# Order of the triples' last products, and another path for two units' transposed k, in an HGRN2 + SwiGLU kernel

## The chip, the cores and the metric

The kernel runs on one core of a Trainium2 chip. The metric is the device time of one execution in microseconds (us), the median of several runs. A profiled execution on the same chip gives the views that are quoted below; its times count from the start of its span. Engines are named PE (TensorE matmuls), PEld (TensorE weight loads), DVE (VectorE), ACT (ScalarE), POOL (GpSimd) and SP (SyncE, which issues DMAs here).

## The reference, cut to what matters

```python
B, H, S, D = 4, 8, 768, 48           # batch, heads, sequence, head size
f = sigmoid(f_logit)
for t in range(S):                   # attention: a decayed state for each head
    state = f[:, :, t, :, None] * state + einsum('bhd,bhe->bhde', k[:, :, t], v[:, :, t])
    y[:, :, t] = einsum('bhd,bhde->bhe', q[:, :, t], state)
x = y.transpose(0, 2, 1, 3).reshape(3072, 384)
g = x @ w_gate                       # 384 x 1536
out = ((g * sigmoid(g)) * (x @ w_val)) @ w_out   # 1536 x 384
```

All inputs and outputs are float32 in value (weights arrive in a wider format and are joined into float32 on the chip).

## The kernel before, in words

**Units and chunks.** The sequence is cut into 6 chunks of 128 positions. A *unit* is one batch entry of one chunk: unit u is chunk u // 4, batch entry u % 4. `attention(u)` is a generator with 15 steps. It turns f, k and q so that features lie on partitions, scans f twice along time on VectorE (`tails` and `gates`), multiplies k by the tails (kT, the *decayed k*) and q by the gates (qT), and then TensorE makes the scores (`sc`, L701), VectorE masks them into `A` (L723), and TensorE makes the output (`y`, L745 and L752) and the state's increment (`dS`, L794). `dS` needs the decayed k with time on partitions again, in the tile `kt`.

**Two ways to kt.** If `turned` (line 634) is false, TensorE transposes kT with the identity into PSUM (L708) and ScalarE copies it out (L721). If it is true, VectorE transposes kT in blocks of 32x32 (L668) into `beside`, which is a part of the room of k, four DMAs write that to a DRAM tile `turn` (L671), and one DMA reads it back as `kt` (L713 or L719). Before, units 5 to 7 and 10 to 19 go through DRAM; units 8 and 9, the first two of the third chunk, use TensorE. From unit 8 on, f, k and q each have one room (`fsquares`, `ksquares`, `qsquares`); `load_after(u, "k")` loads the next unit's k into it when this unit no longer needs the room.

**The MLP.** Chunk 0's tokens go through plain products (`mlp_plain`). Chunks 1 to 5 use a scheme that saves multiplications. `mlp_fifteen(c)` has four *triples* (j = 0, 2, 1, 3) of 15 products each, listed in `PRODUCTS`; each product is one pair of 128x256 results, 0.86 on the planner's clock. In a triple all products named "A" add into one PSUM bank, and likewise "B" and "c":

```python
PRODUCTS = [("A", "a11", "t14"), ("B", "a23", "t8"), ("o", "a21", "b22"),
            ...
            ("A", "a32", "t11"), ("B", "e1", "t3"), ("A", "a22", "b21")]
```

Between two products into one bank ScalarE copies the bank (`c` or `aside`, L1066), VectorE adds or subtracts these copies (L960, L963), ScalarE applies SiLU (L1077) and VectorE multiplies (L1013). Two A banks alternate between triples, B has one bank, and "o" and "c" share two. After the triples come seven products with w_out (`down_seven`), of two parts each: one, six, two, three, four, five, seven. The sums of weights that the scheme needs are made by VectorE in `weight_sums` and those of w_out by ScalarE and accumulating DMAs in `down_weight_sums` (L1000, L1001).

**The order.** A planner merges everything: the MLP's pieces run in sequence and each has a length; attention steps, sums and weight pieces have due times on that clock, and a step comes in ahead of the first piece that starts at or after its due time. `SCORES` says when each unit's scores come and in which kind of bank, `CHAINS` when its preparing steps come; `JOINS_AT`, `SIZES_AT`, `FETCHES_AT`, `EARLY`, `SUMS_AT`, `LATE_SUMS_AT` and `DOWN_SUMS_AT` are due times. What is recorded that way is the order of each engine's own instructions. During the MLP of chunk c the scores of chunk c+1 are made; a unit's scores are put together with the previous unit's `y` and `dS`, so that y, dS, y, sc stand in one block.

**Weights.** Each of 18 weight pieces is fetched, then split by ScalarE (`sizes`, L491 to L495) and joined by VectorE (L505 to L516). A piece in the set `SIGNED` has one more ScalarE instruction and one less on VectorE.

Of the kernel before, what the change touches and what calls it, by code (L numbers as in the profile page):

```python
# [9 lines left out]
FP32 = mybir.dt.float32  # L10
# [10 lines left out]
def general_path(ctx, tc, q, k, v, f_logit, moe_w_gate, moe_w_val, moe_w_out, out):  # L21
# [111 lines left out]
    def attention(u):  # L133
# [22 lines left out]

        A = att.tile([128, H, C], FP32, tag="A", name="A")
        sc = aps.tile([128, 2, 512], FP32, tag="a", name="sc0")
        for a in range(HP):
            for par in range(2):  # L160
# [4 lines left out]
        nc.gpsimd.tensor_tensor(qT, q0, fT, ALU.mult)  # L165
        nc.vector.tensor_tensor(A, sc.rearrange("p r (a t) -> p (r a) t", t=C),
                                ident.unsqueeze(1).broadcast_to((128, H, C)), ALU.mult)
# [4 lines left out]
        for i, m in enumerate(LEVELS):  # L172
# [6 lines left out]
            for a in range(HP):  # L179
# [11 lines left out]
            nc.vector.copy_predicated(  # L191
                A.rearrange("p g (n two r) -> p g n two r", two=2, r=m)[:, :, :, 1, :],
                masks[m].rearrange("p (n r) -> p n r", r=m).unsqueeze(1).broadcast_to((128, H, n, m)),
# [5 lines left out]
        for a in range(HP):  # L199
# [4 lines left out]
            for par in range(2):  # L204
                nc.tensor.matmul(both[:, par * D:(par + 1) * D], lhsT=A[:, par * HP + a, :], rhs=vt[u][:, 2 * a + par, :],
                                 start=(c == 0), stop=True, skip_group_check=True)
# [84 lines left out]
def short_path(ctx, tc, ident, least, judge, q, k, v, f_logit, moe_w_gate, moe_w_val, moe_w_out, out):  # L291
# [9 lines left out]
    nc = tc.nc  # L301
    B, H, S, D = q.shape
    C = 128
    NCH = S // C
    HP = H // 2
# [10 lines left out]
    SQUARES = 2  # L316
# [3 lines left out]
    att = ctx.enter_context(tc.tile_pool(name="att", bufs=1))  # L320
# [77 lines left out]
    NI = C // Q  # L398
    RUN = NI * D

    rooms = {nm: t.rearrange("p n h w -> p (n h w)")[:, 0:Q + HP * RUN] for nm, t in both_raw.items()}
# [127 lines left out]
    NW = 2  # L529
    FIRST = 2  # L530
    NPART = 2
    SIGNED = (0, 1, 4, 6, 7, 8, 9, 11, 15, 16, 17)

    def add_piece(dst, src, parts=1):
        fetch, *rest = weight_piece(dst, src, parts, len(fetches) in SIGNED)
        fetches.append(fetch)
# [39 lines left out]
    def attention(u):  # L576
        b, c = units[u]
# [7 lines left out]
        in_squares = by_squares(u)  # L585
# [37 lines left out]
        else:  # L623
            p = transposed("fTp", fr)
# [6 lines left out]
            load_after(u, "f")  # L631
        yield

        turned = SQUARES * B + 2 <= u < (NCH - 1) * B or c < SQUARES and in_squares
        turn_queue = nc.sync if c >= SQUARES else nc.gpsimd
        kT = att.tile([128, HP, C], FP32, tag="kT", name="kT")
        qT = att.tile([128, HP, C], FP32, tag="qT", name="qT", bufs=2)
# [1 line left out]
        if in_squares:  # L639
            kp = qT.rearrange("p a t -> p (a t)")  # L640
            nc.vector.transpose(parted(kp), split_squares("k"))
            if not turned:
                load_after(u, "k")
        yield

        n = HP * N1
        owner["tail", rot] = owner["start"] = u
        owned(u, ("gate", rot))
        for part in parts:
            at = slice(part.start * N1, part.stop * N1)  # L650
            nc.vector.tensor_tensor_scan(tail[:, at][:, ::-1], gate[:, at][:, ::-1], floor[:, at][:, ::-1], 1.0,
                                         op0=ALU.mult, op1=ALU.max)
        whole = pairs(tail)[:, :, 1:2]
# [10 lines left out]
        if turned:  # L664


            beside = rooms["k"][:, 0:HP * C].rearrange("p (i m) -> p i m", i=NI)
            nc.vector.transpose(beside.rearrange("p i (a e) -> p a i e", e=Q), kT.rearrange("p a (i e) -> p a i e", e=Q))  # L668
            turn = turn_pool.tile([Q, NI, HP, NI, Q], FP32, tag="turn", name="turn")
            for r in range(NI):  # L670
                turn_queue.dma_start(out=turn[:, :, :, r, :].rearrange("t i a e -> t (i a) e"),  # L671
                                  in_=beside[Q * r:Q * (r + 1)].rearrange("t i (a e) -> t (i a) e", e=Q))
            load_after(u, "k")
        yield

        if in_squares:

            (nc.scalar.copy if c >= SQUARES else nc.vector.tensor_copy)(least[:, u, :], whole.rearrange("p a t -> p (a t)"))
            whole = least[:, u, :].unsqueeze(2)
# [12 lines left out]
            decay()  # L692
        yield

        A = att.tile([128, 2, HP, C], FP32, tag="A", name="A")
        sc = [score_bank(u) for _ in range(2)]
        for a in range(HP):
            for par in range(2):
# [6 lines left out]
        if c < NCH - 1 and not turned:  # L705
            p = bank("kt")
# [15 lines left out]
        for par in range(2):  # L722
            nc.vector.tensor_tensor(A[:, par], sc[par].rearrange("p (a t) -> p a t", t=C),  # L723
                                    causal.unsqueeze(1).broadcast_to((128, HP, C)), ALU.mult)
# [9 lines left out]
        if c and b < B - 1:  # L734
# [8 lines left out]
            for par in range(2):  # L743
                for a in range(HP):
                    nc.tensor.matmul(place(a, par), lhsT=v_[:, 2 * a + par, :], rhs=A[:, par, a, :],  # L745
                                     start=a < 2, stop=False, skip_group_check=True)
# [20 lines left out]
        else:  # L767
# [15 lines left out]
            for par in range(2):  # L783
                for n in range(DM // Q):
                    h = n // per * 2 + par
                    at = n * Q - h * D
# [4 lines left out]
        if c < NCH - 1:  # L791
            p = bank("dS")
# [16 lines left out]
    def load_after(u, what):  # L809

        if u + 1 < len(units) and u + 1 != SQUARES * B:
            load(u + 1, what)
# [89 lines left out]
    NJ = NG // 128  # L902

    PRODUCT, DOWN, PLAIN, PLAIN_DOWN = 0.86, 3.9, 2.57, 2.65
# [7 lines left out]
    def chain(k, q, qmul, turn=None, head=None):  # L912
        return (*[k + t for t in STEPS], turn or k + 3.5, head or k + 3.5, q, qmul)

    whole = NJ * TRIPLE + 7 * DOWN
    between = [n * TRIPLE - 0.05 for n in range(NJ)]
    down = [NJ * TRIPLE + n * DOWN / 2 - 0.05 for n in range(14)]
    SCORES = {c: scores for c, scores in zip(range(2, NCH), (
        ((12, "b"), (between[2], "o"), (down[2], "A"), (down[5], "A")),
        ((PRODUCT - 0.05, "b"), (between[1], "o"), (between[3], "o"), (down[3], "A")),  # L920
        *[((down[10] - whole, "A"), (between[1], "o"), (between[3], "o"), (down[3], "A"))] * (NCH - 4)))}
    CHAINS = {c: chains for c, chains in zip(range(2, NCH), (
        (chain(2.6, 4, 8.6), chain(14.5, 20, 23), chain(30, 37, 43.2), chain(57.4, 57.8, 61)),
        (chain(-12, -8.5, -5), chain(3.5, 6, 9), chain(16, 28, 33, 21.5, 23.5), chain(40.1, 53, 55, 44.5, 52)),
        *[(chain(-19.4, -11.2, -9.5), (-7.5, -6.3, 1.3, 2.2, 3.2, 5.5, 8, 10), chain(16, 28, 33, 21.5, 23.5), chain(40.1, 53, 55, 44.5, 52))] * (NCH - 4)))}
    LAST = 72.5

    def times(c):
        at = [t for t, _ in SCORES[c]]
# [6 lines left out]
    def score_bank(u):  # L936
# [3 lines left out]
            return bank("sc")  # L940
        return {"o": banks_o, "A": banks_a}[kind].tile([128, 512], FP32, tag=kind, name="sc")

    JOINS_AT = (0.8, 4.5, 5, 7.6, 13.2, 16.3, 20.3, 27.2, 29.6, 36.1, 38.7, 43.3, 46.6, 47.8, 55.3, 55.4, 67.6, 70.8)
    SIZES_AT = (0.39, 2.4, 6.2, 11.1, 13.2, 18.4, 18.6, 22.1, 31.8, 38, 39.8, 40.1, 43.1, 50.8, 53, 56, 64.8)
    FETCHES_AT = (-1.1, 0.6, 5.5, 5.9, 6, 9.2, 10.6, 21.1, 23.6, 27, 35.5, 35.5, 37.8, 42.4)
    EARLY = (
        (-1.01, 4.17, 4.58, 9.7, 9.87, 10.5, 11, 11.5, 12, 13.4, 17.3, 22, 28.4, 28.41, 33),
        (26, 31.3, 32.8, 34.3, 34.6, 34.6, 36.1, 37.4, 38.2, 40.6, 43.3, 43.4, 50.8, 54.81, 56),
        (46.2, 49.2, 50.7, 51.4, 51.5, 57, 57.6, 58, 62, 63.9, 64.4, 65.5, 68.2, 68.21, 70),
        (63, 64, 66.8, 66.9, 67.4, 67.9, 68.6, 71.6, 73.3, 75.9, 76, 76.7, 78, 78.41, 80.3))  # L950
    SUMS_AT = (64.3, 64.5, 72.58, 72.7, 74.06, 74.74, 75.3, 75.42, 75.98, 76.02, 76.18, 76.3, 76.66, 76.86,
        77.34, 77.54, 78.22, 78.5, 79.18, 79.86, 81.22, 81.26, 81.26, 81.34, 81.62, 81.9, 81.94, 82.58, 82.58, 82.7,
        83.2)
    LATE_SUMS_AT = (23,)
    FINISH = (3, 5, 6, 7, 9, 10)
    DOWN_SUMS_AT = (5.2, 5.21, 18.8, 18.81, 34.5, 34.51, 43, 43.01)
    sums = {}

    def plus(dst, a, b):
# [31 lines left out]
    def down_weight_sums():  # L991
# [4 lines left out]
        for i in (1, 2, 4):  # L996
# [7 lines left out]
    PRODUCTS = [("A", "a11", "t14"), ("B", "a23", "t8"), ("o", "a21", "b22"),  # L1004
                ("A", "a12", "t2"), ("B", "e3", "b32"), ("o", "e0", "t1"),
                ("A", "e5", "t9"), ("B", "e2", "t5"), ("c", "a13", "b11"),
                ("A", "e4", "t4"), ("B", "a33", "t15"), ("c", "a31", "t10"),
                ("A", "a32", "t11"), ("B", "e1", "t3"), ("A", "a22", "b21")]
# [3 lines left out]
    def lag(f, *args):  # L1012
        lagging.append(lambda: f(*args))  # L1013

    def mlp_fifteen(c):
# [113 lines left out]
        hidden_sums, last = down_seven(c, h)  # L1129
        order = list(range(0, NJ, 2)) + list(range(1, NJ, 2))  # L1130
        pieces = [f for j in order for f in triple(j)]
        half = len(PRODUCTS) * (NJ // 2)
        pieces.insert(half + 12, (0, lambda: lag(hidden_sums, 0)))
        pieces += [(0, finish_late), last[0], (0, lambda: lag(hidden_sums, 1))]
        return token_sums, pieces + last[1:]

    def down_seven(c, h):
# [66 lines left out]
        def five(part):  # L1204
            if part == 0:
                kept["p"] = bank2("o7", "o")
            add(kept["p"], of_h(1), b12, True, part)
            if part:
                lag(plus, kept["u"], kept["u"], kept["p"])
                lag(plus, kept["o", 1][:, :, DH:DM], kept["u"], kept["p5"])  # L1210
                lag(plus, kept["o", 1][:, :, 0:DH], kept["u"], kept["p4"])
                for n in range(2):
                    lag(put_out, 1, n, nc.scalar)

        def six(part):
            if part == 0:
# [75 lines left out]
            sizes.pop(0)()  # L1292
        run(b - 1, 4)
    first_join = joins.pop(0)
    first_join(("clamp"))
    sizes.pop(0)()
    run(B - 1, 3)
    first_join(("add"))
    joins.pop(0)()
    next(first[B - 1])  # L1300
    sizes.pop(0)()
# [2 lines left out]

    waiting = [(t, sizes.pop(0)) for t in SIZES_AT]
    waiting += [(t, joins.pop(0)) for t in JOINS_AT]
# [127 lines left out]
```

## Time and profile before

| What | Value |
|---|---|
| Median of 3 runs | 595.06 us (595.02 to 595.18) |
| The profiled execution's own time | 595.19 us |
| Its span, first to last instruction | 593.5 us |
| Granted TensorE clock | 0.998 |
| Busy: PE, DVE, ACT, POOL | 583.6, 477.1, 303.2, 112.2 us |
| Instructions | 11514 |

The span leaves out about 1.7 us around the profiled execution. A busy share is an average over the whole span; the stretches differ. In the timeline each row is a start, a length, an engine, a line, the operation, the tile written and the tiles read, and in brackets how long the engine stood idle before it and what ended that. Lengths of matmuls are modelled, so the distance between starts is the better measure of TensorE's pace.

### The profile page before, as it was taken

Reading aid. Unit: us, or ns where it says so; the run is one execution under the profiler, and the core shown is the slowest. Engines: PE = TensorE matmul, PEld = TensorE weight load, DVE = VectorE, ACT = ScalarE, POOL = GpSimd, SP = SyncE. Lnnn points to the kernel's source line nnn. Section 1 sums busy time; section 2 is a strip of 40 time slices with the busy share of each in tenths; the row PEclk is TensorE's granted clock in tenths of the full one; section 3 lists DMA queues with packets and bytes.
Section 4 is the critical chain, followed back from the end, with each engine's and each line's share of the span. In section 5 each row is a group of like instructions: output and inputs, shape, how many; then the busy total and the mean of one; then the engine's idle time right before and its main releaser. Section 6 shows DMA issues by size and latency. Waiting matters only on the chain.

```text
span 593.5 us, 11514 instructions
## 1 busy us (share of the span) xinstructions
PE 583.6 (98%) x4292; PEld 480.6 (81%) x4292; DVE 477.1 (80%) x826; ACT 303.2 (51%) x567; POOL 112.2 (19%) x240
## 2 busy tenths in 40 slices
PE   8899999999999999999999999999999999999996
PEld 5744445667888999888899888899988899988896
DVE  7978898999989877998986988994978971666631
ACT  3588686024877422676640666631476730355600
POOL 3140345202132240111130030330030330000000
PEclk9999999999999999999999999999999999999999
DMA  9999597333666565552445332544230100100001
GB/s 193 266 309 263 167 229 171 64 99 107 120 120 110 93 149 138 130 109 65 88 117 137 100 81 63 103 109 113 81 92 27 29 11 6 54 1 2 2 0 57
DMA packets 106294, 61.91 MB, mean 104 GB/s; under 512 B 64200, under 2 KB 97032, under 8 KB 106232
## 3 DMA queue, kind: packets, MB, share of 16 engines
q1 hardware_dynamic: 93800, 45.96, 31.8%
q0 software_dynamic: 10992, 13.19, 10.0%
q10 hardware_dynamic: 1440, 1.97, 0.9%
q8 instruction: 35, 0.57, 0.4%
q14 instruction: 27, 0.22, 0.1%
HBM read 47.64 MB, written 8.13 MB: 94 GB/s over the span
## 4 chain that ended last, share of the span: by engine, by line
PE 96%; DVE 2%; ACT 0%; issue 0%; DMA 0%; ACTq 0%; DVEq 0%
PE o L1160 19%; PE A L1061 18%; PE B L1061 15%; PE o L1061 6%; PE c L1061 6%; PE o L868 5%; PE gate L845 5%; PE val L845 5%; PE o L1223 3%; PE sc L701 3%; PE y L745 2%; PE y L774 2%; PE dS L794 2%; PE y L752 1%; PE sc L704 1%; PE kt L708 1%
## 5 line engine op out<-in xcount | busy, mean ns | idle before, releaser
L763 POOL DMA_DIRECT2D xT<-yT x120 | 59.6, 504 | 66.6 <-ACT yT L756 51.4
L1061 PE MATMUL A<-xs,w_both 128*128 128x256 f32 x240 | 62.2, 382 | 0.0
L1160 PE MATMUL o<-w_out,h 128*128 128x192 f32 x360 | 62.0, 327 | 0.0
L1160 PEld LDWEIGHTS o<-w_out,h 128*128 128x128 f32 x360 | 58.7, 190 | 1.2 <-issue 0.7
L1066 ACT COPY aside<-A 128x512 f32<-128x512 f32 x60 | 35.1, 585 | 33.0 <-PE A L1061 32.7
L1066 ACT COPY c<-A 128x512 f32<-128x512 f32 x40 | 23.3, 582 | 55.8 <-PE A L1061 55.8
L960 DVE TENSOR_TENSOR c<-c,aside 128x512 f32<-128x512 f32 x60 | 41.1, 685 | 12.7 <-ACT aside L1066 11.1
L1061 PEld LDWEIGHTS A<-xs,w_both 128*128 128x128 f32 x240 | 44.9, 190 | 6.9 <-issue 1.0
L1013 DVE TENSOR_TENSOR h<-h,c 128x256 f32<-128x256 f32 x100 | 40.5, 413 | 7.6 <-ACT h L1077 7.3
L963 DVE TENSOR_TENSOR c<-c,aside 128x512 f32<-128x512 f32 x60 | 40.9, 682 | 2.8 <-ACT aside L1066 2.8
L1077 ACT ACTIVATE h<-c 128x256 f32<-128x256 f32 x100 | 39.4, 417 | 5.0 <-DVE c L960 3.8
L1160 PE MATMUL o<-ws,h 128*128 128x192 f32 x240 | 41.5, 328 | 0.0
L1061 PE MATMUL B<-xs,w_both 128*128 128x256 f32 x160 | 41.3, 380 | 0.0
L1061 PE MATMUL A<-xs,extra 128*128 128x256 f32 x160 | 41.2, 380 | 0.0
L1061 PE MATMUL B<-xT,extra 128*128 128x256 f32 x160 | 41.1, 379 | 0.0
L1061 PE MATMUL c<-xT,w_both 128*128 128x256 f32 x160 | 41.1, 379 | 0.0
L723 DVE TENSOR_TENSOR A<-sc,causal 128x512 f32<-128x512 f32 x48 | 30.8, 681 | 11.9 <-PE sc L701 11.6
L1066 ACT COPY aside<-B 128x512 f32<-128x512 f32 x60 | 35.1, 585 | 9.0 <-PE B L1061 7.0
L1160 PEld LDWEIGHTS o<-ws,h 128*128 128x128 f32 x240 | 39.1, 190 | 0.7 <-issue 0.7
L963 DVE TENSOR_TENSOR c<-o,c 128x512 f32<-128x512 f32 x40 | 27.3, 684 | 10.9 <-ACT h L1077 6.2
L960 DVE TENSOR_TENSOR c<-c,o 128x384 f32<-128x384 f32 x15 | 8.2, 548 | 34.4 <-PE o L1160 34.4
L1061 PEld LDWEIGHTS B<-xs,w_both 128*128 128x128 f32 x160 | 30.2, 190 | 4.6 <-ACT c L1066 0.4
(165 smaller groups left out, 1211.2 us busy)
## 6 DMA issues: line engine op xcount, KB each, us to landing
fsquares<-in_f_logit_dram SPq DMA_DIRECT2D x64, 96.0 KB, 4.0
qsquares<-in_q_dram SPq DMA_DIRECT2D x64, 96.0 KB, 2.4
ksquares<-in_k_dram SPq DMA_DIRECT2D x64, 96.0 KB, 2.5
w<-in_moe_w_gate_dram SPq DMA_DIRECT2D x6, 768.0 KB
w<-in_moe_w_val_dram SPq DMA_DIRECT2D x6, 768.0 KB, 6.2
w<-in_moe_w_out_dram SPq DMA_DIRECT2D x6, 768.0 KB, 8.4
v<-in_v_dram SPq DMA_DIRECT2D x19, 192.0 KB, 2.9
turn<-ksquares SPq DMA_DIRECT2D x40, 64.0 KB, 2.2
```

The costliest lines, as they stand in the source:

```text
L701: nc.tensor.matmul(sc[par][W * half:W * half + W, a * C:(a + 1) * C], lhsT=kT[r, a, W * half:W * half + W], rhs=qT[r, a, :], start=True, s ...
L723: nc.vector.tensor_tensor(A[:, par], sc[par].rearrange("p (a t) -> p a t", t=C), causal.unsqueeze(1).broadcast_to((128, HP, C)), ALU.mult)
L763: (nc.gpsimd if c >= SQUARES else nc.sync).dma_start(out=xT[c][f % 128:f % 128 + n, f // 128, b * C:(b + 1) * C], in_=yT[r:r + n, par, a / ...
L845: nc.tensor.matmul(p, lhsT=w[:, j, i, :], rhs=xT[c][:, i, :], start=(i == 0), stop=(i == KT - 1))
L868: nc.tensor.matmul(p, lhsT=hidden_tile(h, n // 2)[:, n % 2 * 2 + b // 2, b % 2 * C:(b % 2 + 1) * C], rhs=w_out[:, j, :], start=(n == 0), s ...
L960: nc.vector.tensor_tensor(dst, a, b, ALU.add)
L963: nc.vector.tensor_tensor(dst, a, b, ALU.subtract)
L1013: lagging.append(lambda: f(*args))
L1061: nc.tensor.matmul(p[name][:, n, :], lhsT=weights_of[a][:, n, j, :], rhs=tokens[b], start=fresh and n == 0, stop=True, skip_group_check=True)
L1066: nc.scalar.copy(t, p[name])
L1077: nc.scalar.activation(dst, src[:, 0, :], AF.Silu)
L1160: nc.tensor.matmul(p[:, n, :], lhsT=lhsTs[j][:, n * C:(n + 1) * C], rhs=rhs[:, j, :], start=first and j == order[0] and n == 0, stop=j == ...
```

## The change

1. *Order of last products.* For the triples named in a new table `APART`, the last piece of a triple (product 14) and the first piece of the next one (product 0) change places. In chunks 2 to 5 one piece of down product six is taken out of its place and put ahead of the last triple's product 14. Five score times move from `between[n]` to `inside[n]`, which is one product earlier, so that the attention block stands between products 13 and 14.
2. *Units 8 and 9.* `turned` becomes true for them. Unit 8 uses its own tile `A`, made earlier, in place of the room of k for the block transposes, since the next k is loaded as before; unit 9 uses the room of k and loads the next k after that.
3. *Due times.* Many due times move by a few tenths to a few microseconds. One weight sum moves from before chunk 1 to its 8.22. The first two pairs of `DOWN_SUMS_AT` move from 5.2 and 18.8 to 13 and 26.2. Piece 13 takes piece 7's place in `SIGNED`.
4. *Queues.* Two output DMAs of chunk 1 go to POOL's queue in place of ScalarE's.

```diff
-    SIGNED = (0, 1, 4, 6, 7, 8, 9, 11, 15, 16, 17)
+    SIGNED = (0, 1, 4, 6, 8, 9, 11, 13, 15, 16, 17)
...
-        turned = SQUARES * B + 2 <= u < (NCH - 1) * B or c < SQUARES and in_squares
+        turned = SQUARES * B <= u < (NCH - 1) * B or c < SQUARES and in_squares
...
-            if not turned:
+            if not turned or u == SQUARES * B:
                 load_after(u, "k")
...
         if turned:
-            beside = rooms["k"][:, 0:HP * C].rearrange("p (i m) -> p i m", i=NI)
+            if u == SQUARES * B:
+                A = att.tile([128, 2, HP, C], FP32, tag="A", name="A")
+            beside = A[:, 0].rearrange("p a t -> p (a t)") if u == SQUARES * B else rooms["k"][:, 0:HP * C]
+            beside = beside.rearrange("p (i m) -> p i m", i=NI)
...
-            load_after(u, "k")
+            if u != SQUARES * B:
+                load_after(u, "k")
...
-        A = att.tile([128, 2, HP, C], FP32, tag="A", name="A")
+        if u != SQUARES * B:
+            A = att.tile([128, 2, HP, C], FP32, tag="A", name="A")
...
+    inside = [t - PRODUCT for t in between]
...
         ((12, "b"), (between[2], "o"), (down[2], "A"), (down[5], "A")),
-        ((PRODUCT - 0.05, "b"), (between[1], "o"), (between[3], "o"), (down[3], "A")),
-        *[((down[10] - whole, "A"), (between[1], "o"), (between[3], "o"), (down[3], "A"))] * (NCH - 4)))}
+        ((PRODUCT - 0.05, "b"), (between[1], "o"), (inside[3], "o"), (down[3], "A")),
+        *[((down[10] - whole, "A"), (inside[1], "o"), (inside[3], "o"), (down[3], "A"))] * (NCH - 4)))}
...
-        (chain(2.6, 4, 8.6), chain(14.5, 20, 23), chain(30, 37, 43.2), chain(57.4, 57.8, 61)),
+        (chain(2.6, 4.8, 8.6), chain(14.5, 21.7, 23.2, 21.2, 19.6), chain(30, 37, 43.6), chain(57.4, 56.6, 61)),
...
+    APART = {1: (1, 3), 2: (1, 2), **{c: (2,) for c in range(3, NCH - 1)}, NCH - 1: range(1, NJ)}
...
-    LATE_SUMS_AT = (23,)
+    LATE_SUMS_AT = (8.22, 23.43)
     FINISH = (3, 5, 6, 7, 9, 10)
-    DOWN_SUMS_AT = (5.2, 5.21, 18.8, 18.81, 34.5, 34.51, 43, 43.01)
+    DOWN_SUMS_AT = (13, 13.01, 26.2, 26.21, 34.5, 34.51, 43, 43.01)
...
-        half = len(PRODUCTS) * (NJ // 2)
-        pieces.insert(half + 12, (0, lambda: lag(hidden_sums, 0)))
+        for n in APART[c]:
+            at = n * len(PRODUCTS)
+            pieces[at - 1], pieces[at] = pieces[at], pieces[at - 1]
+        pieces.insert(len(PRODUCTS) * (NJ // 2) + 12, (0, lambda: lag(hidden_sums, 0)))
+        if c > 1:
+            pieces.insert(-1, last.pop(2))
         pieces += [(0, finish_late), last[0], (0, lambda: lag(hidden_sums, 1))]
...
-                    lag(put_out, 1, n, nc.scalar)
+                    lag(put_out, 1, n, nc.gpsimd if c == 1 else nc.scalar)
```

The lists `JOINS_AT`, `SIZES_AT`, `FETCHES_AT`, `EARLY` and `SUMS_AT` (one entry fewer) are also changed and are left out here. They reorder VectorE's and ScalarE's instructions during chunk 0 and leave the order of TensorE's as it was there.

## The prediction, made before the changed kernel was run

> **What bounds the kernel now.** I read the busy table first, then the chain that ended last, then the waits, then the timeline around one boundary between two triples.
>
> ```profile
> PE 583.6 (98%) x4292; PEld 480.6 (81%) x4292; DVE 477.1 (80%) x826; ACT 303.2 (51%) x567; POOL 112.2 (19%) x240
> ...
> PE 96%; DVE 2%; ACT 0%; issue 0%; DMA 0%; ACTq 0%; DVEq 0%
> ```
>
> TensorE is the bound: 98% busy, and 96% of the chain. A gain must be a matmul fewer or a hole in TensorE's stream closed; work on the other engines counts only if it makes TensorE wait. The waits hold one hole that repeats (total us, times, longest us):
>
> ```profile
> PEld A L1061 <- ACT aside L1066: 5.0, 19, 0.3
> ```
>
> The timeline of the boundary after a triple's product 13 (B) shows which:
>
> ```profile
> 181.24 1.03 PE L1061 MATMUL B<-xT,extra 128*128 128x256 f32 x4
> 181.49 0.59 ACT L1066 COPY aside<-A 128x512 f32<-128x512 f32 x1
> ...
> 182.13 0.73 PEld L1061 LDWEIGHTS A<-xT,w_both 128*128 128x128 f32 x4 [0.27 <-ACT aside L1066]
> 182.13 1.13 PE L1061 MATMUL A<-xT,w_both 128*128 128x256 f32 x4
> ...
> 182.88 0.84 PEld L1061 LDWEIGHTS A<-xs,w_both 128*128 128x128 f32 x4
> 183.10 1.03 PE L1061 MATMUL A<-xs,w_both 128*128 128x256 f32 x4
> 183.75 0.41 PEld L1061 LDWEIGHTS B<-xs,w_both 128*128 128x128 f32 x2
> 183.96 0.38 PE L1061 MATMUL B<-xs,w_both 128*128 128x256 f32 x1
> ```
>
> Product 14 (`A<-xT`) adds to the bank that product 12 filled, and ScalarE must first copy that bank aside, which ends at 182.08. An undisturbed product takes 183.96 - 183.10 = 0.86 (0.863 as a mean), and its weight load starts 0.21 ahead of it. Here load and matmul start together, and products 13 and 14 take 183.10 - 181.24 = 1.86 instead of 1.726: **0.134 us lost**. Of the 20 last products 18 show this; in the other two the scores and the kt transposes, or `row`, already stand between 13 and 14.
>
> [...]
>
> **Part 1, last products behind other work.** By the instruction order of the changed kernel, chunks 2 to 4 put something between 13 and 14 at all four places, chunk 5 at the three that paid, chunk 1 at one (its second boundary and its end still pay). That is 3x4 + 3 + 1 = 16. What comes between is the next triple's product 0 (0.86), an attention block (about 3.0), or half of down product six (1.95); each exceeds the 0.03 to 0.25 that the copy was late. Gain 16 x 0.134 = **2.14**. Who is late next? Product 0 needs the other A bank, last read by `h<-h,A`, ending 2.1 to 4.0 before the old product 14 starts: enough. Scores 0.97 earlier at inside[1] and inside[3]: the q multiply ended at least 2.9 before them. Six ahead of 14 puts the SiLUs and hidden sums 1.95 later against TensorE: in chunk 3 the sums end at 393.5 and product three starts at 399.99, so 4.5 remain. I take 0 for these, bounds 0 to +0.8.
>
> **Part 2, k turned by VectorE and DRAM for units 8 and 9.** Eight kt transposes leave TensorE:
>
> ```profile
> 151.63 0.66 PE L708 MATMUL kt<-idf,kT 128*128 128x128 f32 x4
> ...
> 152.12 1.03 PE L1061 MATMUL A<-xT,w_both 128*128 128x256 f32 x4
> ```
>
> 0.49 each time. Without them the product after the scores pays its own late load, 0.10 elsewhere (1.13 against 1.03 after the scores at 233.66). So 2 x 0.39 = **0.78** gained. Added on SP: 2 x (4 writes of 0.63 issue and 1 read of 0.57). From block transpose to kt: 0.7 + 2.6 + 2.2 landing + 0.6 + 5.5 (kt's landing on POOL, at most 12.8) = 11.6. Unit 8 is turned near 147 and needed by dS near 167; unit 9 near 162 and 201. Hidden, by 8 at the least. In SP's order q of unit 9, issued at 148.3 before, comes behind unit 8's turn, near 150.3, and is used at 163.3; k of unit 10 moves from 156.4 behind unit 9's turn, to about 166. It lands (median 2.5) near 169, and VectorE wants it at 174.8. If it came later, VectorE's c sums and the SiLUs behind them would queue; slack about 5, cost 0. The masked A of unit 8 must wait until its borrowed tile is read, near 151; it runs at 154.3. Cost 0.
>
> **Part 3, VectorE and ScalarE around chunk 1.**
>
> ```profile
> 138.00:151.00 13.00, 12.89 (x73) 10.78 (x75) 12.83 (x23) 7.62 (x16) 3.23 (x5) 1.00 0.62 151
> 151.00:164.00 13.00, 13.00 (x86) 10.89 (x78) 12.22 (x22) 11.71 (x22) 1.44 (x1) 1.00 0.55 115
> ```
>
> (length; PE, PEld, DVE, ACT, POOL busy.) VectorE is full here and gets two block transposes (0.63 of its stream each) and one weight sum (0.60) that was made before chunk 1. That sum's move helps once:
>
> ```profile
> 138.93 1.03 PE L1061 MATMUL B<-xs,w_both 128*128 128x256 f32 x4
> ...
> 139.41 0.55 DVE L889 COPY ob<-o 128x384 f32<-128x384 f32 x1
> ...
> 140.06 0.45 PE L1061 MATMUL o<-xT,w_both 128*128 128x256 f32 x1
> ```
>
> Product 2 comes 1.13 after product 1, not 0.86, when the output copy ends, and pays 0.08 more after it: 0.35. The copy comes 0.60 earlier less the token sum now ahead of it, 0.33: 0.27. I take 0.30 of the 0.35, bounds 0.1 and 0.35.
>
> Further on, VectorE reaches unit 9's f transpose (153.3) about when it did, since the 0.63 fills the 0.69 it idled there. Unit 9's q multiply then ends near 167.0; its scores, at 168.53 before, come near 167.4. Slack 0.4; unit 8 keeps 0.6 of 1.6. Cost 0, bound +1.0.
>
> ScalarE loses two kt copies (0.59) and its two `ws` negations (1.06 of stream) move to the start of triples 2 and 3. Before, triple 2 lost 0.40 in two waits (158.25, 161.92). Now its c12 copy ends near 157.5 and product 6 is due at 157.7: both gone, -0.40. In triple 3:
>
> ```profile
> 171.56 0.59 ACT L721 COPY kt<-kt 128x512 f32<-128x512 f32 x1
> ...
> 174.27 0.57 ACT L1066 COPY c<-A 128x512 f32<-128x512 f32 x1
> ...
> 175.19 1.03 PE L1061 MATMUL A<-xs,extra 128*128 128x256 f32 x4
> ```
>
> 1.06 in place of 0.47 moves the copy's end from 174.84 to 175.43 on this scale: product 6 about 0.3 late and 0.1 for its load, +0.40. **Net 0**, bounds -0.4 and +0.5.
>
> Chunk 0 reorders VectorE only. The tightest weight join there precedes its product by 3.2, and the piece signs trade one VectorE and one ScalarE instruction between pieces 7 and 13: 0. The two output DMAs of chunk 1 from ScalarE to POOL sit in waits on VectorE; POOL's next tile copies are 14 later: 0. The wait of 0.49 before unit 11's scores (211.53) stays: the same VectorE work stands behind the same sigmoid.
>
> **Sum.** -2.14 - 0.78 - 0.30 + 0 = -3.22. The profiled execution took 595.19 (span 593.5, 1.7 around it); it becomes 591.97. The shown median is 595.06, 0.13 lower, so I forecast **591.9**.
>
> **Rivals.** *A, chunk 1 gives its part back:* VectorE's 1.9 of added work makes scores 8 or 9 wait, or both ScalarE slips stay. For: windows of 12.83 and 12.22 in 13, slack 0.4. Against: the moved sum and the idle 0.69. About 1.1 is lost: 593.0. *B, the wait on `aside` only moves* to the next product or copy: then only 0.78 + 0.30 is won, 594.0. Against: after product 0 the next A use comes two products on, and B's copy has the same distance as before. *C, slower:* k of unit 10, now behind a DRAM write, comes late [...]. It costs nothing until k is 5 late, and beyond that a us each; slower by 0.2% needs 5 + 3.2 + 1.2 = 9.4 late, say 596.6 at 10. Turn writes land in 2.2, so this is remote. *D, the change does less than it says* is out for part 1: the instruction order shows 16 separations.
>
> **Numbers.** Forecast 0.66, A 0.22, B 0.07, C 0.04, more than forecast 0.01. A measurement here tells about 0.2% (1.2 us) from no change. Forecast and A are beyond that, as is little of B: faster 0.90, same 0.06, slower 0.04. The part bounds reach from -3.7 to about -2 (A worse): range 591.1 to 593.4.
>
> **What would show it.** Right: the row `PEld A <- ACT aside` falls from 19 times to about 3; kt transposes from 28 to 20; no wait of `o` near 140; one near product 6 of chunk 1's third triple; spans 590.3. Wrong: a row of TensorE's waits with `sc <- DVE qT` grown over 0.5, VectorE idle at k of unit 10, or product 14 still starting with its load.

## The result, and the profile after

The changed kernel takes **591.8 us** (median of six runs, 591.73 to 592.24), the kernel before 595.08 in the same session (594.97 to 595.26). The ratio is 0.9947, with a 95% interval of 0.9934 to 0.9959. Forecast were 591.9, and 591.1 to 593.4. The profiled execution took 591.74; its span is 590.0, where before it was 593.5.

The busy table and the first line of the chain that ended last, of the kernel after:

```profile
PE 579.9 (98%) x4284; PEld 481.1 (82%) x4284; DVE 478.4 (81%) x828; ACT 301.8 (51%) x565; POOL 114.1 (19%) x242
...
PE 95%; DVE 2%; ACT 1%; issue 1%; DMA 1%; SPq 0%; ACTq 0%; DVEq 0%
```

TensorE is still the bound, with eight matmuls fewer and 3.7 us less of modelled busy time. VectorE has two instructions and 1.3 us more, ScalarE two fewer. In the waits of TensorE's weight loads (total us, times, longest us) the row that had 19 entries is down to two, and one of another tile is new:

```profile
PEld A L1068 <- ACT aside L1073: 0.5, 2, 0.3
...
PEld B L1068 <- ACT aside L1073: 0.3, 1, 0.3
```

(Lines moved: L1061 is now L1068, L1066 is L1073, L960 is L967, L1000 is L1007.) Where something now stands between products 13 and 14, the timeline looks like this, here in the MLP of chunk 3 with the scores of unit 17:

```profile
336.06 1.03 PE L1068 MATMUL B<-xT,extra 128*128 128x256 f32 x4
337.02 1.09 PE L750 MATMUL y<-A,v 128*64 128x128 f32 x16
337.94 0.62 PE L799 MATMUL dS<-v,kt 128*64 128x48 f32 x16
338.50 0.67 PE L757 MATMUL y<-qT,decayed 48*64 48x128 f32 x16
338.98 1.05 PE L706 MATMUL sc<-qT,kT 48*64 48x128 f32 x32
339.97 1.13 PE L1068 MATMUL A<-xT,w_both 128*128 128x256 f32 x4
340.93 1.03 PE L1068 MATMUL A<-xs,w_both 128*128 128x256 f32 x4
```

Product 14 (`A<-xT`) comes after the attention block. It pays a late weight load (340.93 - 339.97 = 0.96 against 0.86). The product that stood after the scores in the kernel before paid as much (343.61 - 342.64 = 0.97), so nothing is lost by that; the 0.134 at the old place is gone.

The stall at the output copy is gone too. Product 2 (`o<-xT`) follows product 1 after 0.86, where it took 1.13, and product 3 follows it after 0.87, where the 0.08 was paid:

```profile
138.93 1.03 PE L1068 MATMUL B<-xs,w_both 128*128 128x256 f32 x4
139.79 1.03 PE L1068 MATMUL o<-xT,w_both 128*128 128x256 f32 x4
140.66 1.03 PE L1068 MATMUL A<-xs,w_both 128*128 128x256 f32 x4
```

Two new waits stand in chunk 1. Product 6 of the third triple starts at 173.93, together with its weight load, and so does product 1 after the third boundary, at 182.73:

```profile
173.92 0.73 PEld L1068 LDWEIGHTS A<-xs,extra 128*128 128x128 f32 x4 [0.50 <-ACT c L1073]
...
182.73 0.73 PEld L1068 LDWEIGHTS B<-xs,w_both 128*128 128x128 f32 x4 [0.30 <-ACT aside L1073]
```

The first was forecast; the second was not.

**Where the time went, by TensorE's own clock.** I compare the start of each unit's scores, and of the last matmul, in the two traces. A difference between two marks is what was won in the stretch between them:

| Start of | before | after | won so far |
|---|---|---|---|
| scores of unit 8 | 150.59 | 150.25 | 0.34 |
| scores of unit 9 | 168.53 | 167.39 | 1.14 |
| scores of unit 10 | 202.14 | 201.01 | 1.13 |
| scores of unit 12 | 233.66 | 232.52 | 1.14 |
| scores of unit 23 | 484.29 | 481.53 | 2.76 |
| last matmul | 588.18 | 584.99 | 3.19 |

So chunk 1 gave 1.14 and chunks 2 to 5 gave 2.05. What lies after the last matmul, mostly the landing of the last outputs, was 0.3 shorter in this pair of executions (5.0 in place of 5.3); runs of the same kernel differ by as much (591.73 to 592.24), so I leave it out.

### The profile page after: what moved, and what is told of

Its sections match the earlier page's. It is cut to its first block, busy times and chain, and to the rows that moved or that the text cites. A ratio compares the mean times of both kernels' runs of the same rounds, so it can differ in the third digit from the quotient of the medians.

```text
span 590.0 us, 11512 instructions
## 1 busy us (share of the span) xinstructions
PE 579.9 (98%) x4284; PEld 481.1 (82%) x4284; DVE 478.4 (81%) x828; ACT 301.8 (51%) x565; POOL 114.1 (19%) x242
## 4 chain that ended last, share of the span: by engine, by line
PE 95%; DVE 2%; ACT 1%; issue 1%; DMA 1%; SPq 0%; ACTq 0%; DVEq 0%
PE o L1171 19%; PE A L1068 18%; PE B L1068 14%; PE c L1068 6%; PE o L1068 6%; PE o L873 5%; PE gate L850 5%; PE val L850 5%; PE o L1234 3%; PE sc L706 3%; PE y L750 2%; PE y L779 2%; PE dS L799 2%; PE y L757 1%; PE sc L709 1%
## 5 line engine op out<-in xcount | busy, mean ns | idle before, releaser
L1068 PE MATMUL A<-xs,w_both 128*128 128x256 f32 x240 | 61.8, 380 | 0.0
L1073 ACT COPY aside<-A 128x512 f32<-128x512 f32 x60 | 35.1, 586 | 33.5 <-PE A L1068 33.4
L967 DVE TENSOR_TENSOR c<-c,aside 128x512 f32<-128x512 f32 x60 | 41.1, 686 | 12.4 <-ACT aside L1073 10.8
L1068 PEld LDWEIGHTS A<-xs,w_both 128*128 128x128 f32 x240 | 45.2, 190 | 6.5 <-issue 0.3
L1073 ACT COPY c<-A 128x512 f32<-128x512 f32 x40 | 23.3, 583 | 53.2 <-PE A L1068 53.2
L1068 PE MATMUL A<-xs,extra 128*128 128x256 f32 x160 | 41.2, 380 | 0.1
L1068 PE MATMUL B<-xs,w_both 128*128 128x256 f32 x160 | 41.3, 380 | 0.0
L1068 PE MATMUL c<-xT,w_both 128*128 128x256 f32 x160 | 41.1, 379 | 0.0
L1068 PE MATMUL B<-xT,extra 128*128 128x256 f32 x160 | 41.1, 379 | 0.0
L1073 ACT COPY aside<-B 128x512 f32<-128x512 f32 x60 | 35.1, 586 | 9.4 <-PE B L1068 6.6
L694 POOL MEMSET gates<- 128x4 f32 x24 | 3.7, 153 | 171.1 <-DVE qT L593 166.0
L967 DVE TENSOR_TENSOR c<-c,o 128x384 f32<-128x384 f32 x15 | 8.2, 549 | 33.8 <-PE o L1171 33.8
```

Of the source, the lines that this page charges most:

```text
L967: nc.vector.tensor_tensor(dst, a, b, ALU.add)
L1068: nc.tensor.matmul(p[name][:, n, :], lhsT=weights_of[a][:, n, j, :], rhs=tokens[b], start=fresh and n == 0, stop=True, skip_group_check=True)
L1073: nc.scalar.copy(t, p[name])
```

## The experiments

Theory T: product 14 is held by ScalarE's copy of the bank that product 12 filled; putting work in between removes that, and the turned units and the moved sums give the rest, less one new wait for ScalarE (product 6 of triple 3). The rivals are that the loss belongs to the switch at product 14 whatever ScalarE does, or that the new due times alone bring the gain. Each kernel was timed beside the kernel before, which had medians of 595.07, 595.12, 595.21 and 595.04 in the four sessions. "At the last matmul" means the difference of its start in two traces, which leaves out what comes after it.

### 1. The change without the separations

```diff
-     APART = {1: (1, 3), 2: (1, 2), ...}
+     APART = {c: () for c in range(1, NCH)}
-     inside = [t - PRODUCT for t in between]
+     inside = between
-         if c > 1:
-             pieces.insert(-1, last.pop(2))
```

> The changed kernel with part 1 alone undone: product 14 follows product 13 at every boundary again, and half of down product six stands behind the last triple; units 8 and 9 stay turned by VectorE and all new due times stay. Theory (product 14 is held by ScalarE's copy of the bank that product 12 filled): 15 boundaries pay 0.134 us again, 2.0 in all, so 593.8 us; the row of TensorE's weight loads waiting for that copy is back to 18 or 19 times. Rival (the gain is that of the due times and of the kt transposes, and the separations only rename a wait): within 0.3 of the changed kernel's 591.8.

Measured: 594.26 (594.07 to 594.99), ratio to before 0.9986 (0.9978 to 0.9995). The row is back:

```profile
PEld A L1068 <- ACT aside L1073: 5.2, 20, 0.3
```

From unit 12's scores to the last matmul it loses 2.05 against the changed kernel, the whole gain of chunks 2 to 5. A further 0.37 is lost in chunk 1, which T had not foreseen (it gave 593.8): product 6 of the *second* triple waits.

```profile
156.57 1.03 PE L1068 MATMUL o<-xs,extra 128*128 128x256 f32 x4
157.70 1.13 PE L1068 MATMUL A<-xs,extra 128*128 128x256 f32 x4
```

1.13 apart where 0.86 is undisturbed, and 0.10 for the late load. With product 14 ahead of product 0, ScalarE copies product 0's bank 0.4 later. The first line is of this kernel, the second of the changed one:

```profile
153.32 0.59 ACT L1073 COPY c<-A 128x512 f32<-128x512 f32 x1 [0.30 <-PE A L1068]
...
152.92 0.57 ACT L1073 COPY c<-A 128x512 f32<-128x512 f32 x1
```

Everything behind that copy, the negation of 1.17 included, is 0.4 later too. The separation at the first boundary saves no wait at product 14, but it gives ScalarE that 0.4. (All separations were undone here together; that the 0.37 belongs to the first one is read from these traces.)

### 2. The kernel before with a shorter copy

```diff
- lag(minus, got[31], got[31], aside("A"))
+ part = comb.tile([128, 2, TH], FP32, tag="aside", name="aside", bufs=3)[:, 0:1, :]
+ nc.scalar.copy(part, p["A"][:, 0:1, :])
+ lag(minus, got[31][:, 0:1, :], got[31][:, 0:1, :], part)
```

> The kernel before in its own order, with the copy that ScalarE takes of product 12's bank half as wide (256 of 512 columns, and the subtraction that reads it also: half of that subtraction is left out). Theory: the copy then ends near 181.8 instead of 182.08, before product 14 would start, so all 18 losses of 0.134 go without any change of order: 595.1 - 2.4 = 592.7. Rival (the late weight load belongs to the switch of operands or banks between 13 and 14, not to the copy's length): no change, 595.1.

Measured: 592.99 (592.96 to 593.28), ratio 0.9965 (0.9952 to 0.9979). No product was moved. The copy became half as wide, and so did VectorE's subtraction that reads it, so this kernel leaves out half of that subtraction and its output is not the reference's. The loss at product 14 went:

```profile
181.38 0.37 ACT L1114 COPY aside<-A 128x256 f32<-128x256 f32 x1
...
181.80 0.81 PEld L1061 LDWEIGHTS A<-xT,w_both 128*128 128x128 f32 x4
181.98 1.03 PE L1061 MATMUL A<-xT,w_both 128*128 128x256 f32 x4
182.63 0.84 PEld L1061 LDWEIGHTS A<-xs,w_both 128*128 128x128 f32 x4
182.85 1.03 PE L1061 MATMUL A<-xs,w_both 128*128 128x256 f32 x4
```

The copy ends at 181.75 in place of 182.08; the load runs 0.18 ahead of its matmul again and the next product follows after 0.87. So the copy is the cause, and not the switch; the subtraction, which comes after the copy, is nothing that product 14 waits for. The gain is 2.1 (2.03 at the last matmul), not 2.4: at the ends of the five chunks another, smaller wait takes over.

```profile
PEld o L1162 <- ACT aside L1066: 1.1, 5, 0.2
```

There down product one follows 14 directly and finds product 13's bank still being copied. By the trace, the ends of chunks win about 0.05 each in place of 0.134: 5 x 0.08 is the missing 0.4.

### 3. The kernel before with the separations alone

```diff
+     inside = [t - PRODUCT for t in between]
-         ((PRODUCT - 0.05, "b"), (between[1], "o"), (between[3], "o"), (down[3], "A")),
+         ((PRODUCT - 0.05, "b"), (between[1], "o"), (inside[3], "o"), (down[3], "A")),
...
+     APART = {1: (1, 3), 2: (1, 2), **{c: (2,) for c in range(3, NCH - 1)}, NCH - 1: range(1, NJ)}
...
+         for n in APART[c]:
+             at = n * len(PRODUCTS)
+             pieces[at - 1], pieces[at] = pieces[at], pieces[at - 1]
+         if c > 1:
+             pieces.insert(-1, last.pop(2))
```

> The kernel before with the separations alone (something between products 13 and 14 at 16 boundaries, half of down product six ahead of the last 14), all due times and the turns of units 8 and 9 as before. Theory: -2.0 of 595.1, so 593.0, with chunk 1's third boundary worth nothing. Rival (the separations need the new due times of VectorE and ScalarE, else other waits take their place): 594 or more.

Measured: 592.87 (592.70 to 593.14), ratio 0.9964 (0.9951 to 0.9978), so 2.20 below the kernel before; 2.16 at the last matmul. The new due times are not needed for this part. It even wins 0.13 at chunk 1's third boundary, for which nothing was expected and where the full change wins nothing.

### 4. Units 8 and 9 turned by TensorE again

```diff
- turned = SQUARES * B <= u < (NCH - 1) * B or ...
+ turned = SQUARES * B + 2 <= u < (NCH - 1) * B or ...
```

(Together with unit 8's special cases for `A` and the room of k.)

> The changed kernel with units 8 and 9 turned by TensorE again (eight kt transposes and two ScalarE copies of them more, two VectorE block transposes and their DMAs fewer), everything else as changed. Theory (a kt group costs 0.39 net on TensorE): 0.78 more, 592.6; and since ScalarE's kt copies of 0.59 now stand beside its two negations of 1.06 at the start of triples 2 and 3, up to two more waits of 0.4 each, so 592.6 to 593.4. Rival (VectorE was the limit of chunk 1 and the turns cost what they save): 591.8 or below.

Measured: 593.53 (593.39 to 594.03), ratio 0.9975 (0.9966 to 0.9984), slightly above the expected range; the last matmul is 1.43 later than with the change. By unit 10's scores it is 1.45 late: 0.78 for the two kt groups, 0.18 at product 6 of triple 2, and in triple 3 0.38 at product 4 and 0.11 more at product 6:

```profile
172.03 1.03 PE L1067 MATMUL A<-xs,w_both 128*128 128x256 f32 x4
173.17 1.13 PE L1067 MATMUL B<-xT,extra 128*128 128x256 f32 x4
174.14 1.03 PE L1067 MATMUL o<-xs,extra 128*128 128x256 f32 x4
175.37 0.92 PE L1067 MATMUL A<-xs,extra 128*128 128x256 f32 x3 [0.21 <-ACT c L1072]
```

With kt on TensorE, ScalarE's kt copy stands beside its negation there, and both are ahead of the copies that TensorE waits for. Turning the two units through VectorE and DRAM is worth 0.78 on TensorE and, with the negations where the change puts them, nearly as much again (0.67) in waits for ScalarE.

### 5. The waits that were left

The moments of the weight sums; the sigmoid of unit 11; and both, once with a further exchange in chunk 1.

```diff
- DOWN_SUMS_AT = (13, 13.01, 26.2, 26.21, 34.5, 34.51, 43, 43.01)
+ DOWN_SUMS_AT = (1.7, 1.71, 13, 13.01, 39.5, 39.51, 43, 43.01)
```

> The changed kernel with six of the eight moments at which chunk 1's weight sums and negations are made moved to where ScalarE has time (the negations away from the starts of triples 3 and 4). Theory (ScalarE's 1.06 us negation at those two places is what makes product 6 of triple 3 wait 0.37 and the product after the third boundary wait 0.17): both waits go, 591.8 - 0.54 = 591.3. Rival (those waits belong to the exchange of products 14 and 0, or to the SiLU chain alone): 591.8, the waits still there.

Measured: 591.27 (591.20 to 591.37), ratio 0.9934 (0.9920 to 0.9947), 0.53 earlier at the last matmul. Both waits are gone. In triple 3, product 6 again follows product 5 after 0.87:

```profile
172.80 1.03 PE L1068 MATMUL o<-xs,extra 128*128 128x256 f32 x4
173.67 1.03 PE L1068 MATMUL A<-xs,extra 128*128 128x256 f32 x4
```

```diff
- *[t - 0.01 for t in at[1:]]
+ at[1] - 0.01, 53.5 if c == 2 else at[2] - 0.01
```

> The changed kernel with one due time changed: unit 11's sigmoid at 53.5 instead of 55.44, so that VectorE begins its part of unit 11 about 1.9 us earlier. Theory (the wait of 0.48 before unit 11's scores is the VectorE work behind that sigmoid): 0.37 to 0.48 less, 591.3 to 591.4. Rival (VectorE is held there by something else, or work displaced by the move is late next): 591.8 or more.

Measured: 591.50 (591.30 to 591.86), ratio 0.9937 (0.9924 to 0.9951), 0.44 earlier at the last matmul. Of the changed kernel:

```profile
209.51 0.67 PE L757 MATMUL y<-qT,decayed 48*64 48x128 f32 x16
210.39 1.10 PE L706 MATMUL sc<-qT,kT 48*64 48x128 f32 x32 [0.21 <-DVE qT L593]
```

and with the earlier sigmoid:

```profile
209.52 0.67 PE L757 MATMUL y<-qT,decayed 48*64 48x128 f32 x16
210.00 1.05 PE L706 MATMUL sc<-qT,kT 48*64 48x128 f32 x32
```

Both together, and `APART[1] = (1, 2, 3)`:

> The two due-time changes together (weight sums where ScalarE has time, unit 11's sigmoid earlier), and product 14 of chunk 1's second triple also behind the next triple's product 0. Theory: the gains add, -0.54 - 0.4 - 0.13 = -1.1, so 590.7, about 4.4 below the kernel before. Rival (the moved work makes another wait on VectorE or ScalarE): 591.2 or more.

Measured: 590.93 (590.76 to 591.30), ratio 0.9929 (0.9916 to 0.9943). The two due-time changes alone:

> The changed kernel with the two due-time changes alone (weight sums at the starts of triples 1, 2 and 4 and later in 4, unit 11's sigmoid at 53.5), product 14 of chunk 1's second triple back at its place. The kernel that also moved that product gained 0.99 where 1.1 was expected, and in its trace unit 9's scores came 0.13 earlier but the product after them 0.12 later. Theory (that product, behind unit 9's scores, only finds another wait): -0.53 - 0.44 of 591.8, so 590.8, equal to the other within 0.1. Rival (the 0.12 was lost elsewhere): 590.9 to 591.0, 0.1 above it or more.

Measured: 590.98 (590.75 to 591.08), ratio 0.9931 (0.9917 to 0.9945). The two medians are equal within 0.05, though both are some 0.2 above what was expected, and both kernels reach 0.99 at the last matmul. So the due-time changes add (0.53 + 0.44), and the further exchange is worth nothing: product 14 leaves its wait and the scores of unit 9 come 0.13 earlier, but take 1.10 to the next product in place of 0.98. What in the scores is late there stays open. The version with the two due times beats both kernels: it is 4.06 below the kernel before in its session, and some 0.8 below the change, which was timed in another session.

### 6. How much more VectorE work fits ahead of units 8 and 9

```diff
- nc.vector.transpose(...)
+ for _ in range(4 if u == SQUARES * B else 1):
+     nc.vector.transpose(...)
```

> The changed kernel with unit 8's block transpose on VectorE made four times instead of once (the same result): three times 0.63 us more of VectorE's stream, 1.9 us, where the prediction put the risk of the added turns. Theory (units 8 and 9 keep 0.64 and 0.59 us of slack between the end of the q multiply and the scores, and VectorE has next to no idle time before them): 1.9 - 0.6 = 1.3 us later, 593.1, with the wait at unit 8's scores. Rival 1 (VectorE has hidden slack ahead of chunk 1's scores): 591.8. Rival 2 (no slack at all, VectorE bounds this stretch): 593.7.

Measured: 594.20 (593.92 to 595.97), ratio 0.9985 (0.9979 to 0.9992); 2.19 later at the last matmul, more than any theory gave. The four take 2.94, so three more cost 2.24, 0.75 each:

```profile
145.26 2.94 DVE L672 STREAM_TRANSPOSE A<-kT 128x512 f32<-128x512 f32 x4
```

At unit 8's scores the count holds: the room between q multiply and scores shrinks by 0.73 (from 0.79 to 0.05, some 0.09 more than had been counted as usable), 2.24 less that is 1.51, and they start 1.50 later.

```profile
148.43 1.03 PE L1069 MATMUL A<-xs,w_both 128*128 128x256 f32 x4
149.75 1.13 PE L1069 MATMUL B<-xT,extra 128*128 128x256 f32 x4 [0.30 <-ACT aside L1074]
151.75 1.10 PE L707 MATMUL sc<-qT,kT 48*64 48x128 f32 x32 [0.87 <-DVE qT L593]
```

Then 0.69 more is lost in triple 2, at products 4 and 6. These wait for ScalarE, and ScalarE for VectorE's sums. To see whether that begins at once, one transpose more:

```diff
+ for _ in range(2 if u == SQUARES * B else 1):
```

> The changed kernel with unit 8's block transpose on VectorE made twice (the same result): 0.75 us more of VectorE's stream, the price of one that the kernel with three more showed (2.24 for three). Theory 1 (the slack that counts is the 0.64 of the q multiply before unit 8's scores): 0.1 lost at most, 591.9. Theory 2 (VectorE's sums also feed ScalarE's copies and SiLUs, and behind ScalarE's 1.06 us negation at the start of triple 2 the copy for product 6 has only about 0.2 to spare): product 6 of triple 2 waits about 0.5 and pays 0.1 for its late weight load, so about 592.4.

Measured: 592.53 (592.41 to 592.57), ratio 0.9953 (0.9939 to 0.9966); 0.67 later at the last matmul, as Theory 2 has it. Unit 8's scores are on time to 0.01. Product 4 of triple 2, which no theory had named, loses 0.21 and product 6 0.48:

```profile
154.84 1.03 PE L1069 MATMUL A<-xs,w_both 128*128 128x256 f32 x4
155.81 1.13 PE L1069 MATMUL B<-xT,extra 128*128 128x256 f32 x4
156.78 1.03 PE L1069 MATMUL o<-xs,extra 128*128 128x256 f32 x4
158.01 1.13 PE L1069 MATMUL A<-xs,extra 128*128 128x256 f32 x4 [0.21 <-ACT c L1074]
```

ScalarE's part of the same kernel:

```profile
151.22 0.59 ACT L1074 COPY aside<-B 128x512 f32<-128x512 f32 x1 [1.09 <-DVE c L968]
151.82 1.28 ACT L619 ACT_TABLE_LOAD   x1
153.12 0.63 ACT L619 ACTIVATE fsquares<-fsquares 128x512 f32<-128x512 f32 x1
153.66 0.57 ACT L1074 COPY c<-A 128x512 f32<-128x512 f32 x1
154.12 1.17 ACT L1008 ACTIVATE ws<-w_out 128x1152 f32<-128x1152 f32 x1
155.19 0.57 ACT L1074 COPY c<-B 128x512 f32<-128x512 f32 x1
155.78 1.28 ACT L1085 ACT_TABLE_LOAD   x1
...
157.40 0.57 ACT L1074 COPY c<-A 128x512 f32<-128x512 f32 x1
```

It stood idle 1.09 for a VectorE sum, where the changed kernel's trace has 0.35, and then ran without a gap to the copy at 157.40 that product 6 needs; that copy started at 156.66 in the changed kernel. Two table loads of 1.28 each are in that chain; each of them takes longer here than the negation (1.17).

The same transpose, with the negation taken out of that chain:

```diff
- DOWN_SUMS_AT = (13, 13.01, 26.2, 26.21, 34.5, 34.51, 43, 43.01)
+ DOWN_SUMS_AT = (1.7, 1.71, 39.5, 39.51, 41.2, 41.21, 43, 43.01)
```

> The same second block transpose, and the negations moved away from the starts of triples 2, 3 and 4 (to the start of triple 1 and to triple 4's middle and end). Theory 2: without the negation ahead of it, the copy for product 6 of triple 2 has about 1.2 to spare, so the added VectorE work costs nothing there, and the waits of triple 3 and of the third boundary go as before: 591.3, 1.1 below the kernel with the transpose alone. Theory 1: also 591.3, but then only 0.5 to 0.6 below it.

Measured: 597.73 (597.59 to 598.71), ratio 1.0045 (1.0031 to 1.0059). As a whole it failed, since the edit puts the sums too close together, but its first part still gives an answer. Up to unit 9's scores it is only 0.20 later than the change, where the transpose alone was 0.69: the waits of triple 2 are gone, and the 0.20 are unit 9's own scores, whose slack of 0.59 is less than 0.75. So Theory 2 holds there, with one wait in the next place. What followed was not foreseen: the last sum's negation reads what the DMA of an earlier one has to land first. ScalarE waited 4.14 for that DMA, and TensorE waited with it.

```profile
189.09 1.03 PE L1069 MATMUL c<-xT,w_both 128*128 128x256 f32 x4
193.78 1.81 PE L1069 MATMUL A<-xs,extra 128*128 128x256 f32 x4 [3.67 <-ACT aside L1074]
195.39 1.91 PE L1069 MATMUL B<-xs,w_both 128*128 128x256 f32 x4
197.10 1.23 PE L1069 MATMUL c<-xT,w_both 128*128 128x256 f32 x4
```

## Why the prediction was right

The forecast was 0.1 off, inside its range, and the case that it held likeliest came about. By its own steps, in us of TensorE:

| Step | forecast | measured |
|---|---|---|
| chunks 2 to 5, 15 separations | -2.01 | -2.05 |
| chunk 1's third boundary, the 16th | -0.13 | +0.04 |
| kt of units 8 and 9 off TensorE | -0.78 | -0.79 |
| output copy ahead of product 2 | -0.30 | -0.35 |
| two waits of triple 2 | -0.40 | -0.40 |
| product 6 of triple 3 | +0.40 | +0.37 |
| sum | -3.22 | -3.18 |

The last matmul is 3.19 earlier. That the sum is met to 0.04 is in part luck: the third boundary was missed by 0.17, and four small errors the other way make up most of it. Two slips of arithmetic in the prediction change nothing of this: its sum comes to 591.84 where 591.9 is forecast, and k of unit 10 being 10 us late would, at its own rate, give about 596.8 and not 596.6.

- **Part 1.** Right in size, and its mechanism was tested from both sides: taken out of the change it costs the same 2.05 in chunks 2 to 5, put alone into the kernel before it brings 2.16, and shortening the copy brings most of it with no separation at all. The step "Who is late next? ... enough" failed at one of 16 places. At chunk 1's third boundary product 14 is free, but ScalarE's copy of product 13's bank came at 182.09, after 1.18 of waiting for a VectorE sum, and the following product waited 0.07 and 0.10 for its load. With the weight sums elsewhere (the first kernel of experiment 5) that copy starts at 181.50, which is 0.22 earlier against TensorE, since 0.37 was already won at product 6, and the wait is gone. This is rival B, at one place.
- **What the step missed.** The separation at chunk 1's first boundary counted as nothing, since scores stood there already. Experiment 1 prices it at 0.37: without it ScalarE is 0.4 later, and the gain that the prediction puts down to the moved negation ("both gone, -0.40") would nearly all be lost again. The sum came out right because both edits were in the change; that the first boundary's separation was one of them was not reckoned with, and that is luck.
- **Part 2.** The -0.78 is met to 0.01. Of the moved DMAs, k of unit 10 was issued at 164.91 where the prediction said about 166, and VectorE used it at 173.77 with no wait for it: rival C did not begin.
- **Part 3.** The 0.27 to 0.35 for the output copy took its upper end. The slack from the q multiply's end to the scores of units 8 and 9 was forecast at 0.6 and 0.4; the trace has 0.79 and 0.74. Some 0.15 of that isn't usable, because scores that wait for the q multiply start that much after its end (unit 11's do: 210.24 to 210.39), so 0.64 and 0.59 were left. But slack at the scores was the wrong measure of how close rival A was. Experiment 6 shows that one more 0.75 of VectorE work passes unit 8's scores unharmed and costs 0.67 through ScalarE's copies. The cover that the prediction named was there; the nearest danger stood beside it.
- **The wait before unit 11's scores** stayed, as forecast: with the late load behind it, it cost 0.45 before and 0.44 after, where the prediction had put it at 0.49. Experiment 5 shows that one due time removes it.

## What to carry to other kernels

Look for accumulating matmuls that wait for a copy of their own bank. Here 0.03 of such waiting cost 0.134: the weight load, otherwise 0.21 ahead, started with its matmul, and the next product came after 0.97 in place of 0.86. Work in between won 2.16 at 16 places, a shorter copy 2.03 at 18. Ask of each engine that feeds the bound whether it is late *through another one*: here VectorE's slack at its own consumer was 0.64, and through ScalarE's queue nearly nothing: 0.75 more work on VectorE cost 0.67. Put long instructions of a feeding engine where its next consumer is far away (moving the negations won 0.53), and mind the DMA chain that such sums may form among themselves (4.14 of waiting in the last kernel of experiment 6).

## What was not expected of the hardware

- After the hole of 3.83 us in the last kernel of experiment 6 (from 189.09 + 0.86 to 193.78), the matmuls of 128x256 started 0.427 apart (195.39 to 197.10 are four) and not 0.216. The granted clock that this trace records is 1.00 from 190 to 193, 0.64 from 193 to 197 and 0.94 from 197 to 201. What is missing from 1 there, 4 x 0.36 + 4 x 0.06, gives an estimate of 1.7 us lost on top of the wait itself, nearly half of the hole again. This is one hole; holes of other lengths were not tried.
- Three repeats of a block transpose into one tile took 2.24 more of VectorE, 0.75 each, where one alone lasts 0.70 and takes 0.62 of the stream (145.26 to the next start at 145.88). Whether each waits for the one before it, since they write the same tile, was not tested.
